# Attention with a parallel SwiGLU gate on one core: pacing the FFN groups, filling TensorE lulls with zero-weight matmuls, and splitting the first statistics

## The chip, the core and the metric

The kernel runs on one core of a Trainium2 chip. The metric is the device time of one execution in microseconds, as the median of several runs. The engines are named as in the profile: PE (TensorE matmul), PEld (weight load), DVE (VectorE), ACT (ScalarE), POOL (GpSimd), SP (SyncE, which issues most DMAs).

## The reference

The input `x` has 2048 tokens of width 512, in bf16. It is layer-normalised once; the result feeds an attention block with 32 query heads of width 16 that share one key and one value head, and a SwiGLU FFN with hidden width 1792. The attention's output is gated with the silu of the FFN's output and added to `x`.

```python
xn = layernorm(x)
q = (xn @ wq) as 32 heads of 16;  k = xn @ wk;  v = xn @ wv
s = (softmax(q k^T / 4) v, heads joined) @ wo
f = (silu(xn @ w_gate) * (xn @ w_up)) @ w_down
out = x + s * silu(f)
```

## The kernel before

The queries are cut into 4 chunks of 512 tokens, the heads into 4 groups of 8. A pair (chunk, head group) has two halves, and a half of a pair is a *block*: 32 blocks in all. A block handles 4 heads against 16 key tiles of 128 keys. For each key tile and each two heads there is one *tile* of scores, 128 keys by 1024 (two heads of 512 queries), so there are 1024 tiles.

Scores are made by PE with 32-row matmuls, two for a tile (`sc_emit`, L814), into one of three 1024-wide PSUM rings. Rings 0 and 1 go to ACT, which turns a tile into probabilities with one exponential (L865). Ring 2 goes to DVE, which makes an approximate exponential in four instructions for two tiles (L892 per tile, then L905, L908, L910 per pair of tiles). 778 tiles go to ACT and 246 to DVE. The product with the values (PV, `pv_emit`, L697) is a *column group*: four 32-column matmuls, one for each head, accumulated in the bank `o_ps` over a block. At the end of a block DVE copies the bank to SBUF (`oev`, L710). The matmul that comes last in the emission carries the stop flag, and the copy waits for all of the block's PV groups.

Between these, PE works off column groups of another kind (`grp_pe`, `cmm`, L466): the gate and up projections (`g_ffn`), the down projection (`g_down`), the q projections of later pairs (`g_q`) and the output projections of finished chunks (`g_out`). All of them use the one bank `m_ps`, whose next user waits for `m_rel`. A gate column block has a tanh on ACT (L608, L625 for the down projection), and multiplications on DVE.

The order on every engine is made in advance, by a planner that runs when the kernel is built. It keeps a clock for each engine with assumed durations (an exponential 0.904 us, a column group 0.215 us), picks the next operation, and at the end emits all operations in the order of their planned starts, chained on each engine. On the chip each engine follows that order; only semaphores decide when. `pump` decides when a job (an FFN column block, a q projection, an output projection) becomes available; `pe_pick` decides what PE does next: a score tile for ACT (`ts`), another ready operation (`tm`, chosen by `rank`), or a score tile for DVE (`td`). Before the DVE share begins, gaps of PE are filled with junk matmuls into an unused bank (L1102). `F0` and `F1` are the tile numbers between which the FFN jobs are spread.

At the start, `pro_x` handles a chunk of 512 tokens: DVE takes the mean and variance of four 128-token tiles (L415, L416), POOL the power -1/2 (L422), DVE normalises (L425), PE transposes (L430), and the result is copied to `xnT` (L436). Chunk 0 goes in two steps of two tiles, with the copies on ACT, followed by the k and q projections of 256 tokens each (L439). All of `x` is loaded by SP's queue, the k, q and v weights by ACT's.

At the end, chunk 3 has no time to go through the usual output path. `g_part` queues the output projection of its four token tiles over the first three head groups, 12 column groups into four banks, once all 1024 tiles are issued. `g_h0` normalises the first half of the last pair by transposes on PE (L940) and three DVE instructions (L948 to L950). The same is done for the second half after the last block's copy; then come two more transposes with a copy on ACT (L1179, L1181), the last quarter of the projection, and the gating and addition (L641, L646). A range check of the denominators and of `v` (`g_checks`, L970 to L974) leads to a flag that would start an exact second path at the end; with this data it does not run.

Of the kernel before, what the change touches and what calls it, by code (L numbers as in the profile page):

```python
# [8 lines left out]
FP32 = mybir.dt.float32  # L9
BF16 = mybir.dt.bfloat16  # L10
# [4 lines left out]
ALU = mybir.AluOpType  # L15
# [17 lines left out]
F_ON, F_OFF = 26, 60  # L33
PB_URG, R_FILL = 6, 0.8
TOL, MERGE = 0.12, 0.1
# [233 lines left out]
def kernel(  # L269
# [64 lines left out]
    def sb(shape, dtype, name):  # L334
        return wp.tile(shape, dtype, name=name)
# [33 lines left out]
    dn = sb([P, NPAIR, GRP], FP32, "dn")  # L369
    rc = sb([P, NPAIR, GRP], FP32, "rc")  # L370
    dscr = [dpool.tile([8, 512], FP32, name=f"dscr{i}") for i in range(2)]
    o_tok = sb([P, 4, P], BF16, "o_tok")
    dl = sb([P, 2, 4, 4, 1], FP32, "dl")
    rd = sb([P, 2, 4, 4, 1], FP32, "rd")
    dlc = sb([P, 32], FP32, "dlc")
    fmin = sb([P, 4], FP32, "fmin")
    fm2 = sb([P, 2], FP32, "fm2")

# [8 lines left out]

    for n in range(0, 4, 2):
        nc.sync.dma_start(out=x_sb[:, n:n + 2, :], in_=x_v[:, n:n + 2, :])
    with nc.allow_non_contiguous_dma(reason="tiny k/v weight loads (32B rows)"):  # L390
# [3 lines left out]
    for c in range(1, NSC):  # L394
# [6 lines left out]
    COEF = (CE, CW)  # L401
    nc.vector.memset(QB[1][:], 0.0)
    chain("POOL", nc.gpsimd.tensor_copy(out=wk_rep[:].rearrange("p k (r d) -> p k r d", d=DH),
                                        in_=wk_sb[:].rearrange("p k (o d) -> p k o d", o=1).to_broadcast(
# [93 lines left out]
    def pro_x(c, pr, banks, ev_eng):  # L498
        arrive = ext(XARR[min(c, 7)])
        step, pk = (2, 1) if c == 0 else (4, 2)  # L500
        evs, grp = [], []
        for n0 in range(4 * c, 4 * c + 4, step):
            st = None
            for n in range(n0, n0 + step):
                st = OP("DVE", 0.77, [arrive, st], lambda n=n: e_stats(n), (pr, n, 0), name="stat")
            v = OP("DVE", 0.08, [st], lambda a=n0, b=n0 + step: e_veps(a, b), (pr - 0.07, n0, 1), name="veps")
            r = OP("POOL", 0.7 + 0.08 * (step - 2), [v], lambda a=n0, b=n0 + step: e_rstd(a, b), (0,), name="rstd")
            for n in range(n0, n0 + step):
                xo = OP("DVE", 0.33, [r, xr_rel[n % 4]], lambda n=n: e_xn(n), (pr - 0.15 if c == 0 else pr - 0.05, n),
                        name="xn")  # L510
                bk = banks[n % 4 // pk]
                h = n % pk
                t_ = OP("PE", 0.26, [xo, brel[bk]] + grp, lambda n=n, bk=bk, h=h: e_tr(n, bank[bk], h), (pr, n), "f",
                        "tr")
                xr_rel[n % 4] = t_
                grp = grp + [t_]
                if len(grp) == pk:
                    ev = OP(ev_eng, 0.5 if ev_eng == "ACT" else 0.34 if pk == 1 else 0.6, grp,
                            lambda n=n, bk=bk: e_txe(n + 1 - pk, pk, bank[bk], ev_eng), (pr - 0.1, n), name="txe")
                    if c:  # L520
                        held.append((grp[0], ev, bk))
                    grp = []
                    brel[bk] = ev
                    evs.append(ev)
        return evs
# [137 lines left out]
    def norm_pair(pair, d0, d1, ev1):  # L663
# [3 lines left out]
        def pack():  # L667
            return [nc.sync.dma_start(out=o0[GRP * g + DH:GRP * g + GRP, :], in_=o1[GRP * g + DH:GRP * g + GRP, :])
                    for g in range(4)]
        pk = OP("DMA", 2.4, [d0, ev1], pack, (0,))  # L670
        r = OP("DVE", 0.26, [d0, d1], lambda: nc.vector.reciprocal(out=rc[:, pair, :], in_=dn[:, pair, :]), (2.2,),
               name="recip")
        sc_ = dscr[pair % 2]
        w = OP("DMA", 2.2, [r], lambda: nc.sync.dma_start(out=sc_[:].rearrange("h (c q) -> (h c) q", q=GRP),
                                                          in_=rc[:, pair, :]), (0,))
        rbt = rb[pair % 2]
# [64 lines left out]

    pair_blk = []

# [189 lines left out]
    F0, F1 = min(F_ON, NTILE), max(NTILE - F_OFF, min(F_ON, NTILE) + 1)  # L933
    job = {"f": 0, "acc": 0.0, "q": 1, "o": 0, "chk": False, "h0": False, "part": False}
    LB = NBLK - 1
# [40 lines left out]

    def g_part():
        order = sorted((0, 1), key=lambda i: slot[i].seq)
        st["late"], st["last"] = order
        bks = ["2a", "2b", "m", f"{order[0]}a"]  # L980
        st["obank"] = bks
        for n, bk in enumerate(bks):
            rel = slot[2] if bk[0] == "2" else (m_rel[0] if bk == "m" else slot[order[0]])
            for jj in range(NQ - 1):
                OP("PE", MMF, [rel, o_ready3()], lambda n=n, bk=bk, jj=jj: e_out_mm(LN + n, bank[bk][:, :D], [jj]),
                   (3,), "c", "part")

    def o_ready3():
        return kb_ready.get(("mul", NPAIR - 2))

    def pump(now):
# [7 lines left out]
        if job["f"] == len(ffn_list) and not job["h0"] and planned([oev.get(LB - 1)]):  # L999
            job["h0"] = True  # L1000
            g_h0()
            return
        if job["h0"] and not job["part"] and p == NTILE and cur["pair"] is None:
            job["part"] = True
            g_part()
            return
# [6 lines left out]
        if n < 4 * (NSC - 1) and n // 4 in o_ready and planned([o_ready[n // 4], g_ready.get(n)]) \  # L1013
# [3 lines left out]
            return  # L1017
        if job["f"] < len(ffn_list) and job["acc"] / tot * (F1 - F0) + F0 <= p:
            w, fn = ffn_list[job["f"]]
            job["f"] += 1  # L1020
            job["acc"] += w
            fn()

    def pe_pick():
# [20 lines left out]
        if ready:  # L1045
# [6 lines left out]
            def rank(o):  # L1052
# [7 lines left out]
                if o.name == "part":  # L1060
                    return (4, o.prio)
                return (R_FILL, (o.seq,))
            co = min(now, key=lambda o: (rank(o), o.seq))
# [20 lines left out]
        if junk and T - F > 0.3:  # L1084
            return F, ("junk", None)
        if ts is not None and ts <= T + 1e-9:
            return ts, ("act", i)
# [7 lines left out]
    def pe_do(start, what):  # L1095
        kind, arg = what
        if kind == "op":
            sd.run(start, arg)
            return
        if kind == "junk":  # L1100
# [65 lines left out]
    def tadd(eng, ins):  # L1166
        chain(eng, ins)

    la, lb = st["late"], st["last"]
    tq01, tq23 = ring[lb][:, 0:512], ring[lb][:, 512:1024]  # L1170
    tp = [ring[la][:, 512:1024], o_ps[:]]
    tadd("PE", tq_emit(1, [0, 1], tq01))
    tadd("PE", tq_emit(1, [2, 3], tq23))
    oTl = oT[(NSC - 1) % 2]
    for h, src in ((0, tq01), (1, tq23)):
# [13 lines left out]
    for k in range(2):  # L1189
        tadd("PE", e_out_mm(LN + k, obk[k], [NQ - 1]))  # L1190
    tadd("PE", nc.tensor.transpose(out=tq01[0:1, 0:P], in_=fmin[:, 3:4], identity=ident_f[:]))
    for k in range(2, 4):
# [9 lines left out]
    tadd("DVE", e_out_mul(LN + 1, obk[1], dsts[1]))  # L1202
    tadd("DVE", nc.vector.tensor_reduce(out=fm2[0:1, 0:1], in_=tq01[0:1, 0:P], axis=AX.X, op=ALU.min))
    tadd("DVE", e_out_mul(LN + 2, obk[2], dsts[2]))
    fin_add(2, nc.gpsimd, "POOL")
    tadd("DVE", nc.vector.tensor_single_scalar(out=fm2[0:1, 1:2], in_=fm2[0:1, 0:1], scalar=0.5, op=ALU.is_lt))
    fin_add(1, nc.vector, "DVE")
    tadd("DVE", nc.vector.tensor_copy(out=flag_i[:], in_=fm2[0:1, 1:2]))
    tadd("DVE", e_out_mul(LN + 3, obk[3], dsts[3]))
# [38 lines left out]
```

## Time and profile before

| | before |
|---|---|
| median of 8 runs | 793.44 us (791.13 to 795.14) |
| profiled execution: time | 796.25 us |
| profiled execution: span, first to last instruction | 794.5 us |
| mean granted TensorE clock | 0.977 |
| busy: PE / DVE / ACT / POOL | 723.9 / 740.8 / 757.5 / 51.3 us |
| ACT exponentials (L865) | 778, 737.1 us |
| scores on PE (L814) | 2048 matmuls, 319.1 us |
| PV groups on PE (L697) | 1556 + 492 + 492 matmuls |

A row of the costliest groups gives line, engine, operation, tiles and shapes, then the count, the busy time, the mean of one, and the idle time of the engine ahead of it with what ended it. Successive ACT instructions overlap in their records, so the mean of one is longer than the distance between two; the distance is taken from their starts. The ends of matmuls are modelled. In a view by windows each engine has its busy time in the window and the number of its instructions; the granted clock is a share of full speed.

### The profile page before, as it was taken

The numbers are of one execution on the slowest core, as the hardware profiler recorded it, in microseconds if no ns is written. First come the engines' busy times: TensorE is split into PE (matmuls) and PEld (weight loads), VectorE is DVE, ScalarE is ACT, GpSimd is POOL, SyncE is SP. The second block draws the span as 40 slices with busy tenths as digits, with TensorE's granted clock in tenths as the row PEclk, the third lists the DMA queues.
The fourth block names the chain that finished last, engine by engine and source line by source line (L and its number), as shares of the span: only waits on it lengthen the run. The fifth ranks groups of instructions, "written<-read, shape, count | busy, mean of one in ns | idle before, by whom it ended". The sixth has DMA issues, their size and how long they took to land.

```text
span 794.5 us, 19255 instructions
## 1 busy us (share of the span) xinstructions
PE 723.9 (91%) x7968; PEld 217.0 (27%) x7968; DVE 740.8 (93%) x925; ACT 757.5 (95%) x860; POOL 51.3 (6%) x59
## 2 busy tenths in 40 slices
PE   8988899999899899998999899999999989999984
PEld 3322222222222222222222222222222222222221
DVE  7789999999999999999999989999999999999983
ACT  5899999999999999999999989999999999999991
POOL 3200000000012000000003000000001100000001
PEclk9899999999999999999999989999999999999996
DMA  9300000000010000000000000000001000000001
GB/s 331 109 2 7 17 2 23 1 10 15 2 30 22 22 2 8 17 1 23 3 22 22 16 14 2 23 2 8 17 2 29 21 23 2 9 16 1 23 1 31
DMA packets 19463, 18.49 MB, mean 23 GB/s; under 512 B 8552, under 2 KB 15464, under 8 KB 19368
## 3 DMA queue, kind: packets, MB, share of 16 engines
q1 hardware_dynamic: 17496, 16.37, 6.8%
q8 instruction: 64, 1.05, 0.6%
q10 hardware_dynamic: 1872, 0.82, 0.4%
q14 instruction: 31, 0.25, 0.1%
HBM read 12.62 MB, written 2.34 MB: 19 GB/s over the span
## 4 chain that ended last, share of the span: by engine, by line
PE 36%; ACT 29%; DVE 22%; issue 8%; DMA 1%; SPq 1%; POOL 0%; DVEq 0%; ACTq 0%
ACT Pb L865 24%; PE ring L814 15%; PE m_ps L466 13%; DVE Ub L892 8%; PE o_ps L697 7%; DVE Wb L910 4%; ACT th L608 4%; DVE Wb L905 3%; DVE Eb L908 2%; ACT th L625 1%; SPq L724 1%; DMA dn<-oa 1%; DVE stats L415 1%; DVE ab L610 1%; DVE ab L641 1%
## 5 line engine op out<-in xcount | busy, mean ns | idle before, releaser
L865 ACT ACTIVATE Pb<-ring 128x1024 bf16<-128x1024 f32 x778 | 737.1, 1171 | 12.1 <-PE ring L814 11.5
L814 PE MATMUL ring<-QB,KT 32*128 32x512 bf16 x2048 | 319.1, 384 | 46.3 <-ACT Pb L865 40.6
L892 DVE TENSOR_SCALAR Ub<-ring 128x1024 uint16<-128x1024 f32 x246 | 299.5, 1218 | 15.6 <-PE ring L814 10.9
L814 PEld LDWEIGHTS <-KT 32*128 32x128 bf16 x2048 | 104.6, 91 | 356.9 <-issue 352.8
L910 DVE TENSOR_TENSOR Wb<-Wb,Ub 128x2048 f16<-128x2048 f16 x123 | 151.2, 1230 | 0.0
L697 PE MATMUL o_ps<-Pb,VA 128*32 128x512 bf16 x1556 | 150.3, 391 | 0.2 <-DVE oa L710 0.2
L905 DVE TENSOR_SCALAR Wb<-Ub 128x2048 uint16<-128x2048 uint16 x123 | 87.5, 712 | 0.3
L908 DVE TENSOR_SCALAR Eb<-Ub 128x2048 uint16<-128x2048 uint16 x123 | 86.9, 709 | 0.0
L466 PE MATMUL m_ps<-xnT,wg_sb 128*32 128x512 bf16 x896 | 74.7, 391 | 0.6 <-DVE QB L593 0.5
L466 PE MATMUL m_ps<-wd_sb,hT 128*32 128x512 bf16 x896 | 72.9, 383 | 0.5 <-DVE g_sb L627 0.5
L466 PE MATMUL m_ps<-xnT,wu_sb 128*32 128x512 bf16 x896 | 71.4, 392 | 0.7 <-DVE ab L610 0.6
L682 POOL TENSOR_TENSOR oT<-oa,rb 128x512 bf16<-128x512 f32 x15 | 21.2, 1410 | 622.4 <-DMA rb<-dscr 387.7
L697 PE MATMUL o_ps<-Eb,VD 128*32 128x512 f16 x492 | 48.9, 387 | 5.4 <-DVE Eb L908 4.3
L697 PEld LDWEIGHTS <-VA 128*32 128x32 bf16 x1556 | 37.9, 94 | 53.8 <-issue 53.4
L697 PE MATMUL o_ps<-Wb,VD 128*32 128x512 f16 x492 | 49.0, 388 | 2.2 <-DVE Wb L910 1.7
L697 PEld LDWEIGHTS <-VD 128*32 128x32 f16 x984 | 29.2, 94 | 48.2 <-issue 47.1
L608 ACT ACTIVATE th<-m_ps 128x512 f32<-128x512 f32 x56 | 41.6, 743 | 0.0
L614 DVE TENSOR_TENSOR hT<-ab,m_ps 128x512 bf16<-128x512 f32 x56 | 38.1, 681 | 2.3 <-PE m_ps L466 2.2
L610 DVE SCALAR_TENSOR_TENSOR ab<-th,m_ps 128x512 f32<-128x512 f32 x56 | 38.1, 680 | 1.3 <-ACT th L608 1.0
L710 DVE COPY oa<-o_ps 128x512 f32<-128x512 f32 (+1 forms) x33 | 22.0, 670 | 9.3 <-PE o_ps L697 9.0
L466 PEld LDWEIGHTS <-wg_sb 128*32 128x32 bf16 x896 | 17.1, 95 | 26.3 <-issue 25.3
L466 PEld LDWEIGHTS <-wu_sb 128*32 128x32 bf16 x896 | 16.1, 95 | 26.3 <-issue 24.3
(94 smaller groups left out, 235.4 us busy)
## 6 DMA issues: line engine op xcount, KB each, us to landing
rb<-dscr SPq DMA_DIRECT2D x15, 256.0 KB
dn<-oa SPq DMA_DIRECT2D x120, 2.0 KB, 1.7
oa<-oa SPq DMA_DIRECT2D x60, 32.0 KB, 2.0
wg_sb<-in_B_w_gate_dram SPq DMA_DIRECT2D x1, 1792.0 KB, 11.4
wu_sb<-in_B_w_up_dram SPq DMA_DIRECT2D x1, 1792.0 KB
wd_sb<-in_B_w_down_dram SPq DMA_DIRECT2D x1, 1792.0 KB, 20.3
out_dram<-xn SPq DMA_DIRECT2D x14, 128.0 KB, 1.7
x_sb<-in_A_x_dram SPq DMA_DIRECT2D x3, 512.0 KB
```

The costliest lines, as they stand in the source:

```text
L466: return [nc.tensor.matmul(out=dst[GRP * j:GRP * j + GRP, :], lhsT=w[:, GRP * j:GRP * j + GRP], rhs=rhs, start=start, stop=stop, tile_posi ...
L608: t_ = OP("ACT", 0.477, [a], lambda: nc.scalar.activation(out=th[i][:], in_=m_ps[:], func=ACT.Tanh, scale=0.5), (0,), name="tanh")
L610: s_ = OP("DVE", 0.6, [t_, ab_rel[i]], lambda: nc.vector.scalar_tensor_tensor(out=ab[i][:], in0=th[i][:], scalar=1.0, in1=m_ps[:], op0=ALU ...
L614: h = OP("DVE", 0.6, [b], lambda: nc.vector.tensor_tensor(out=hT[:, f, :], in0=ab[i][:], in1=m_ps[:], op=ALU.mult), (1,), name="hmul")
L697: r.append(nc.tensor.matmul(out=o_ps[GRP * g:GRP * g + GRP, :], lhsT=lhs, rhs=rhs, start=(n == 0), stop=(n == pv_total[(b, g)] - 1), tile_ ...
L710: oev[b] = sd.new(_Op("DVE", 0.6, [], lambda: [nc.vector.tensor_copy(out=oat[:, a:z], in_=o_ps[:, a:z]) for a, z in cuts], (0.2,), name="o ...
L814: return lambda: [nc.tensor.matmul(out=ring[sl][:, u * 512:(u + 1) * 512], lhsT=KT[half][GRP * g:GRP * g + GRP, t * P:(t + 1) * P], rhs=QB ...
L865: lambda: nc.scalar.activation(out=Pb[pi][:], in_=ring[i][:], func=ACT.Exp, scale=escale, bias=ebias),
L892: lambda: nc.vector.tensor_scalar(out=Ub[ui][:, x * 1024:(x + 1) * 1024], in0=ring[2][:], scalar1=ubias, scalar2=UINF, op0=ALU.add, op1=AL ...
L905: o1 = OP("DVE", 0.6, [pa, pa0, w_rel[u - NE] if u >= NE else None], lambda: nc.vector.tensor_scalar(out=Wb[ei][:], in0=Ub[ui][:], scalar1 ...
L908: o2 = OP("DVE", 0.6, [pa, pa0, e_rel[u - NE] if u >= NE else None], lambda: nc.vector.tensor_scalar(out=Eb[ei][:], in0=Ub[ui][:], scalar1 ...
L910: o3 = OP("DVE", 1.135, [o1, o2], lambda: nc.vector.tensor_tensor(out=Wb[ei][:].bitcast(FP16), in0=Wb[ei][:].bitcast(FP16), in1=Ub[ui][:]. ...
```

## The change

- **Start.** The second half of chunk 0 of `x` is loaded by ACT's queue, ahead of the weights, instead of SP's. Its statistics are made by ACT: two copies that accumulate the sum, the mean, two squares of `x - mean` that accumulate the variance, with `hT` as a scratch output. DVE then makes `veps` from the sums. The first half stays on DVE.
- **Pacing.** `ahead()` is the number of FFN column groups queued beyond the even spread. An FFN job becomes available as soon as this is 16 or less (`AHEAD`), where before it had to be zero or less. While it is 8 or more (`LAZY`), the rank of such groups goes from 0.8 to 3.5, behind PV.
- **Zero groups.** In `pe_pick`, if the next planned start is at least one column group away and fewer than seven (`ZN`) column groups started in the last 3.4 us of planned time, a column group with weights `zw` (all zero) and the first 512 tokens of `xnT` is put into the PV bank of the open block, provided that the block has begun and has PV groups still to come.
- **Tail.** The partial projection goes into four separate pieces: token tiles 0 and 1 (bank of ring 2) are made available when the last DVE tile is issued, tile 2 (`m_ps`) after the half-0 normalisation is queued, tile 3 after the last transposes.
- **Flag.** The minimum over the partitions is replaced by a matmul with a column of ones, and the flag is one comparison instead of three DVE instructions.
- **Reciprocals.** `rc` keeps two slots instead of one for each pair.

```diff
-PB_URG, R_FILL = 6, 0.8
+PB_URG, AHEAD, LAZY, ZN = 6, 16, 8, 7
...
-    for n in range(0, 4, 2):
-        nc.sync.dma_start(out=x_sb[:, n:n + 2, :], in_=x_v[:, n:n + 2, :])
+    nc.sync.dma_start(out=x_sb[:, 0:2, :], in_=x_v[:, 0:2, :])
+    nc.scalar.dma_start(out=x_sb[:, 2:4, :], in_=x_v[:, 2:4, :])
...
+            if c == 0 and n0 == 2:
+                a = None
+                for n in (2, 3):
+                    a = OP("ACT", 0.55, [arrive, a], lambda n=n: nc.scalar.activation(
+                        out=hT[:, n, :], in_=x_sb[:, n, :], func=ACT.Copy, accum_out=ssum[:, n - 2:n - 1]), (-1,),
+                        name="asum")
+                a = OP("ACT", 0.2, [a], lambda: nc.scalar.activation(
+                    out=mv[:, 2:4, 0], in_=ssum[:, 0:2], func=ACT.Copy, scale=1.0 / D), (-1,), name="amean")
+                for n in (2, 3):
+                    a = OP("ACT", 0.55, [a], lambda n=n: nc.scalar.activation(
+                        out=hT[:, n, :], in_=x_sb[:, n, :], func=ACT.Square, scale=-1.0, bias=mv[:, n, 0:1],
+                        accum_out=ssum[:, n:n + 1]), (-1,), name="asq")
+                v = OP("DVE", 0.08, [a], lambda: nc.vector.tensor_scalar(
+                    out=veps[:, 2:4], in0=ssum[:, 2:4], scalar1=1.0 / D, scalar2=EPS, op0=ALU.mult, op1=ALU.add),
+                    (pr - 0.07, n0, 1), name="veps")
...
-    def g_part():
...
+    def g_part(n):
+        bk = st["obank"][n]
+        rel = slot[2] if bk[0] == "2" else m_rel[0]
+        for jj in range(NQ - 1):
+            OP("PE", MMF, [rel, o_ready3()], lambda jj=jj: e_out_mm(LN + n, bank[bk][:, :D], [jj]), (3,), "c", "part")
...
+    def ahead():
+        return job["acc"] - (cur["issued"] - F0) * tot / (F1 - F0)
...
-        if job["h0"] and not job["part"] and p == NTILE and cur["pair"] is None:
+        if not job["part"] and act_block() in (LB, None) and cur["pair"] is None and dve_tile(0) is None \
+                and planned([o_ready3()]):
             job["part"] = True
-            g_part()
+            g_part(0)
+            g_part(1)
+        if job["h0"] and not job["partm"] and planned([o_ready3()]):
+            job["partm"] = True
+            g_part(2)
...
-        if job["f"] < len(ffn_list) and job["acc"] / tot * (F1 - F0) + F0 <= p:
+        if job["f"] < len(ffn_list) and ahead() <= AHEAD:
...
-                return (R_FILL, (o.seq,))
+                return (0.8 if ahead() < LAZY else 3.5, (o.seq,))
...
+        zb = act_block()
+        zb = NBLK - 1 if zb is None else zb
+        if not junk and cur["issued"] >= D_START and T - F >= MMF + sd.switch("c") \
+                and sum(1 for q in c_log[-ZN:] if q > F - 3.4) < ZN:
+            for bb in (zb - 1, zb):
+                if bb >= 0 and oev[bb].start is None and oev[bb - 1].start is not None \
+                        and sd.avail(oev[bb - 1], "PE") <= F and blk_pv[bb] and blk_pv[bb][0].start is not None \
+                        and oev[bb].left > 0 and any(o.start is None for o in blk_pv[bb]):
+                    return F, ("zero", bb)
...
+        if kind == "zero":
+            o = _Op("PE", MMF, [oev[arg - 1]], pv_emit(arg, [(zw[:], xnT[:, 0, 0:512], g) for g in range(4)]), (0,), "c",
+                    "zero")
...
     tadd("PE", tq_emit(1, [2, 3], tq23))
+    tadd("PE", e_out_mm(LN + 3, bank[st["obank"][3]][:, :D], range(NQ - 1)))
...
-    tadd("PE", nc.tensor.transpose(out=tq01[0:1, 0:P], in_=fmin[:, 3:4], identity=ident_f[:]))
+    tadd("PE", nc.tensor.matmul(out=tq01[0:1, 0:1], lhsT=fmin[:, 3:4], rhs=ones_f[:], start=True, stop=True))
...
-    tadd("DVE", nc.vector.tensor_reduce(out=fm2[0:1, 0:1], in_=tq01[0:1, 0:P], axis=AX.X, op=ALU.min))
...
-    tadd("DVE", nc.vector.tensor_single_scalar(out=fm2[0:1, 1:2], in_=fm2[0:1, 0:1], scalar=0.5, op=ALU.is_lt))
+    tadd("DVE", nc.vector.tensor_single_scalar(out=flag_i[:], in_=tq01[0:1, 0:1], scalar=P - 0.5, op=ALU.is_lt))
...
-    tadd("DVE", nc.vector.tensor_copy(out=flag_i[:], in_=fm2[0:1, 1:2]))
```

## The prediction

> **What bounds the kernel now.** I read the page first, for the engines' shares and the clock row. ACT is busy 95% of the span, DVE 93%, PE 91%. The clock row is 9 almost everywhere and dips at both ends.
>
> ```profile
> PE 723.9 (91%) x7968; PEld 217.0 (27%) x7968; DVE 740.8 (93%) x925; ACT 757.5 (95%) x860; POOL 51.3 (6%) x59
> PEclk9899999999999999999999989999999999999996
> ```
>
> ACT sets the pace. In the undisturbed stretches its 1024-wide exponentials start 0.915 us apart without a gap, and 778 of them at 0.915 us with 72 tanh steps at 0.49 us come to 747 us. From the first exponential (13.23) to the end of the last (777.23) it is 764.0 us, so about 15 us are lost on ACT in between. Next I cut windows, because the clock row is too coarse. Columns: length, busy time of PE, PEld, DVE, ACT, POOL, granted clock, DMA.
>
> ```profile
> 6.41:9.82 3.41, 2.96 (x22) 1.60 (x21) 3.25 (x13) 1.07 (x2) 1.11 (x3) 1.00 1.15 328
> 306.79:310.20 3.41, 2.41 (x28) 0.74 (x24) 3.41 (x4) 3.41 (x6) 0.00 (x0) 1.00 0.02 5
> 310.20:313.61 3.41, 3.41 (x32) 0.49 (x24) 2.64 (x4) 2.54 (x4) 0.00 (x0) 0.50 0.02 2
> 402.36:405.77 3.41, 3.41 (x30) 0.66 (x26) 1.84 (x4) 2.91 (x5) 0.00 (x0) 0.50 0.01 1
> 463.80:467.21 3.41, 2.52 (x28) 0.78 (x20) 3.41 (x5) 3.41 (x5) 0.47 (x1) 1.00 0.00 0
> 467.21:474.04 6.83, 6.83 (x52) 1.11 (x50) 6.21 (x7) 4.64 (x5) 0.00 (x0) 0.50 0.01 2
> 774.41:781.24 6.83, 6.40 (x56) 2.22 (x59) 0.76 (x2) 2.82 (x4) 0.00 (x0) 0.50 0.01 2
> ```
>
> Three times in mid-kernel the granted clock falls to 0.50 for one or two windows of 3.41 us; each time the window before held few column groups (sets of four 32-column matmuls). It falls again at the very end. In the half-clock windows PE is full and ACT has holes: the bound moves from ACT to PE. ACT's timeline there, with the idle time before each row:
>
> ```profile
> 467.43 1.02 ACT L865 ACTIVATE Pb<-ring 128x1024 bf16<-128x1024 f32 x1 [0.22 <-PE ring L814]
> 468.94 1.02 ACT L865 ACTIVATE Pb<-ring 128x1024 bf16<-128x1024 f32 x1 [0.49 <-PE ring L814]
> 470.46 1.02 ACT L865 ACTIVATE Pb<-ring 128x1024 bf16<-128x1024 f32 x1 [0.49 <-PE ring L814]
> ```
>
> The exponentials come 1.51 us apart instead of 0.915, so each loses 0.6. Summing what exceeds 0.915 (0.49 after a tanh) from the starts gives 1.3 us around 310, 0.9 around 402 and 2.9 around 467: 5.1 us for the three drops. The rest of the 15 us is 5.6 before 45 us, where the clock is 0.50 from 16.65 to 26.89, and 4.5 in scattered stalls.
>
> **Start: half the statistics of chunk 0 to ACT.** The chain of the second half of chunk 0:
>
> ```profile
> 7.39 0.69 DVE L415 BATCH_NORM_STATS2 stats<-x_sb 128x6 f32<-128x512 bf16 x1
> 8.59 0.71 POOL L422 TENSOR_TENSOR rstd<-veps,neg_half 128x2 f32<-128x2 f32 x1 [1.77 <-DVE veps L419]
> 9.33 0.74 DVE L425 TENSOR_SCALAR xn<-x_sb,mv,rstd 128x512 bf16<-128x512 bf16 x2
> 13.23 1.02 ACT L865 ACTIVATE Pb<-ring 128x1024 bf16<-128x1024 f32 x1 [0.48 <-PE ring L814]
> ```
>
> DVE loses two stats (0.69) and two aggregates (0.18). ACT, idle here until 7.97, gets four 512-wide passes and a tiny one. Accumulating activations are not in the trace; the nearest row is ACT's 512-wide copy (two in 1.07 us). Data by 4.2 (issued at 0.72, 3.5 us to landing), four passes at 0.54, 0.2 for the mean and about 0.2 for handovers end at 6.8. Then veps 0.2, POOL 0.71 behind its other power and the k-weight copy. That copy starts about 0.5 later, since the k-weight load now stands behind the x load on ACT's queue; its memsets (1.1 together) push the first power from 5.82 to about 6.2, which is covered because the second ends last. xn of the second half starts near 8.3 instead of 9.33: 1.0 us gained. Twice the copy's time per pass would put ACT at 9.0 and lose 1.2; in DVE's order xn of tiles 0 and 1 now stands behind the veps that waits for ACT, so nothing would cover that.
>
> Against it stands the clock. In the window 6.41 to 9.82 the old program had five full-width junk matmuls beside eight transposes. The new PE order has one junk matmul ahead of the first scores where the old one had nine, and sixteen transposes in a row. If the clock halves there, the sixteen 256-column q and k matmuls (0.107 each by the pitch of the old rows) double, 1.7 us, nearly all of it on this path. Ends +1.0 and -0.7; I take a gain of 0.4, a little above the middle, because the row with the nearest load stayed at 1.00.
>
> The Trainium skill ("TensorE: Matmul & The Clock Gate", Part 4: PE-mode transpose) says that transposes don't count as PE-busy for the clock. No row here has transposes alone. By that rule the start would be the -0.7 and the sum below 1.1 us higher.
>
> **Middle: pacing and zero groups.** A column group may now be queued up to 16 ahead and steps back behind everything when 8 ahead, so the same 1296 groups of the FFN and projections are spread. Where PE still has a lull with fewer than seven groups in 3.4 us, a zero-weight group is put into the open PV bank: 148 matmuls, 37 groups. Exponentials (778), DVE tiles (246) and all evacuations keep their counts. I counted, in both program orders, the places after the first tiles where four ACT tiles in a row have five column groups or fewer: ten before (and the tail), six after. The drops of the trace fell at exponentials 298, 392 and 459; the first two are such places. At two hits in ten places, six places give 1.2 drops where the trace had three; at 1.7 us each 2.0 us stay of 5.1. Gain 3.1; ends 0 and 5.1.
>
> The zero groups cost PE time: consecutive groups stand 0.22 us apart, so 8.1 us in all. PE is recorded busy 671.92 of 725 us between 45 and 770, and the groups go only where the planner sees a hole; the planner counts 0.904 per exponential where the chip takes 0.915, so holes are longer than planned. Bounds 0 and 8.1; I take 0.3, near the hiding end. The last PV evacuation of a block now waits for its zero groups too, but these precede the block's last PV in PE's order.
>
> The skill speaks against this part: the same page ("HAM oscillation — how this bites in real kernels") states as its rule that no PE-idle gap should exceed about 3.4 us. No such gap exists here: PE was busy 2.41 and 2.52 us of the windows ahead of two drops, and the clock fell. The measurement decides: a sparse window is enough. By the rule alone the zero groups would buy nothing and the 3.1 would fall away.
>
> **Tail: the partial out-projection.** The old tail:
>
> ```profile
> 768.59 8.64 ACT L865 ACTIVATE Pb<-ring 128x1024 bf16<-128x1024 f32 x9
> 776.38 2.78 PE L466 MATMUL ring<-wo_sb,oT 128*32 128x512 bf16 x24
> 778.94 0.64 PE L697 MATMUL o_ps<-Pb,VA 128*32 128x512 bf16 x4
> 779.64 0.76 DVE L710 COPY oa<-o_ps 128x256 f32<-128x256 f32 x2 [6.42 <-PE o_ps L697]
> 781.69 0.66 PE L940 MATMUL ring<-ident_f,oa 128*128 128x128 f32 x4
> 782.45 0.17 DVE L948 COPY dl<-ring 128x8 f32<-128x8 f32 x1 [2.06 <-PE ring L940]
> ```
>
> ACT ends at E = 777.23. The last PV stands behind six half-clock out-projection groups, the transposes behind six more, and DVE reads them at E+5.22. In the new order the last PV stands first, then nine groups, then the transposes; the last three groups come after these, where PE waited 0.89 us for o_tok anyway. But the half-0 normalisation (0.17, 0.25, 0.42) now follows the last PV evacuation on DVE, and the m_ps groups wait for it. With a full clock: PV at E+0.2, evacuation E+0.9 to E+1.7, normalisation to E+2.6, three groups (0.65), transposes and handover (0.76): DVE reads at E+4.1. That is 1.1 gained. With a half clock nine groups at 0.43 put it at E+5.3: nothing. The final-flag steps lose two small DVE operations (0.2 and 0.06 on the serial chain). Since the last FFN tanh now stands four ACT steps from the end instead of ten, the last windows are dense and I take the full clock: 1.4 with the flag; ends -0.1 and 1.9.
>
> **Sum.** The profiled execution took 796.25 us, span 794.5 and 1.75 around it. 796.25 - 0.4 - 3.1 + 0.3 - 1.4 = 791.65. It stands 2.8 above the median of 793.44. I read that as drops: the fastest run, 791.13, is the profiled one less the 5.1. So a median run holds about 2.3 us of drops (an estimate), of which the same six tenths, 1.4, go; with the other three terms (-1.5) that is 790.5 us.
>
> **Rivals.** First, the sparse windows only move: six places remain, and the start goes cold. Then the drops stay, the start gives -0.7, the tail 1.4: 793.44 + 0.7 + 0.3 - 1.4 = 793.0. For it: ten such places gave only two hits, so places and drops are loosely tied; against it: four-tile stretches with six groups or fewer fall from 91 to 34. Second, slower: PE is in order, and each zero group or pushed-back FFN group that the chip reaches late stands ahead of the next score pair, which ACT awaits. All 37 late cost 8.1 us: 793.44 - 2.9 + 7.8 = 798.3. It decides from about 21 late groups on (4.5 us: the 2.9 gained and the 1.6 that can be told). For it: PE already makes ACT wait at 15 exponentials after 45 us; against it: those waits sum to 6.3 us and most lie in the drops. Third, better: no drop at all and the full 1.0 at the start, 793.44 - 2.3 - 1.0 + 0.3 - 1.4 = 789.0, or less if spreading also removes some of the 4.5 of scattered stalls.
>
> **Chances.** Forecast 0.52, better 0.14, moved windows 0.22, slower 0.12. About 0.2% (1.6 us) is what a measurement of this kernel can tell from no change. So faster 0.66, same 0.22, slower 0.12. The range runs from 787.3, some of the scattered stalls gone, to 794.8, where the slower case has barely begun.
>
> **What would show it.** Right: no 0.50 windows, or one, between 45 and 770; ACT busy in nearly every window; the first exponential at 12.2 to 13.0; DVE's first read of the last transposes about 4.1 us after ACT's end at clock 1.00. Wrong: half-clock windows near exponentials 82, 108, 131, 322, 472 or 662; ACT waiting for scores right behind zero groups; an ACT statistics chain ending past 8 us; a half clock between 9 and 13 us.

## The result, and the profile after

The change made the kernel slower: 799.07 us median of 21 runs (790.37 to 805.53) against 792.70 of 58 runs of the kernel before on the same chips; ratio 1.0056, 95% interval [1.0036, 1.0076]. The ratios here and below leave out runs that are over 1.5% slower than the fastest of their kernel (6 of 23 of the changed kernel), while medians keep them. The forecast was 790.5. The profiled execution of the changed kernel is one of its fastest, 791.36 us with a span of 789.6, so its trace shows where things stand and not how much a usual run loses; for the sizes the runs are used.

The page, first the shares and then the clock row:

```profile
PE 730.0 (92%) x8110; PEld 222.0 (28%) x8110; DVE 738.0 (93%) x921; ACT 758.9 (96%) x869; POOL 49.0 (6%) x59
PEclk9999999899999999999999999999999999999998
```

PE is busy 6.1 us longer, the zero groups among it. Windows of the changed kernel around half clock (length, busy PE, PEld, DVE, ACT, POOL, granted clock, DMA):

```profile
5.28:8.69 3.41, 1.22 (x6) 0.37 (x4) 1.32 (x8) 2.10 (x7) 2.41 (x7) 1.00 1.05 346
8.69:12.10 3.41, 2.80 (x21) 2.35 (x22) 2.85 (x8) 2.04 (x4) 0.73 (x2) 0.50 1.11 362
121.34:124.75 3.41, 2.15 (x24) 0.71 (x20) 3.15 (x5) 3.41 (x5) 0.00 (x0) 1.00 0.04 7
124.75:128.16 3.41, 3.41 (x28) 0.64 (x26) 2.00 (x4) 2.65 (x3) 0.00 (x0) 0.50 0.19 39
145.23:148.64 3.41, 2.34 (x24) 0.91 (x21) 3.41 (x5) 3.41 (x6) 0.00 (x0) 1.00 0.01 1
148.64:155.47 6.83, 6.82 (x50) 1.21 (x53) 5.33 (x7) 4.91 (x6) 0.00 (x0) 0.50 0.02 3
660.64:664.05 3.41, 2.47 (x24) 0.71 (x25) 3.26 (x5) 3.41 (x5) 0.00 (x0) 1.00 0.03 4
664.05:667.46 3.41, 3.41 (x30) 0.63 (x22) 1.81 (x4) 2.36 (x4) 0.00 (x0) 0.50 0.03 5
```

The drops in mid-kernel are not gone. They stand at exponentials 108, 131 (half clock from 148.64 to 155.47) and 662: three of the six sparse places that the prediction named. In each of the three sparse windows DVE copies the PV bank at a block's end (at 121.47, 145.73 and 660.76). The start goes cold from 8.69 to 12.10, where the old program had full clock. The start in the timeline (start, length, idle time before the row in brackets):

```profile
4.32 0.63 ACT L510 ACTIVATE hT<-x_sb 128x512 bf16<-128x512 bf16 x1 [1.58 <-DMA x_sb<-in_A_x_dram]
4.86 0.19 ACT L510 ACTIVATION_READ_ACCUMULATOR hT<-x_sb 128x1 f32 x1
...
6.28 0.61 POOL L407 COPY wk_rep<-wk_sb 128x512 bf16<-128x512 bf16 x1 [4.93 <-DMA wk_sb<-in_A_wk_dram]
...
7.47 0.34 DVE L519 TENSOR_SCALAR veps<-ssum 128x2 f32<-128x2 f32 x1 [1.28 <-ACT hT L516]
...
8.52 1.54 DVE L429 TENSOR_SCALAR xn<-x_sb,mv,rstd 128x512 bf16<-128x512 bf16 x4 [0.71 <-POOL rstd L426]
...
14.08 2.90 ACT L887 ACTIVATE Pb<-ring 128x1024 bf16<-128x1024 f32 x3 [0.57 <-PE ring L836]
```

All four normalisations now wait to 8.52; the old program had the first two at 6.75. The first exponential comes at 14.08, not 13.23. The tail, in the same view:

```profile
771.55 3.14 ACT L887 ACTIVATE Pb<-ring 128x1024 bf16<-128x1024 f32 x3
...
774.74 0.39 PE L719 MATMUL o_ps<-Pb,VA 128*32 128x512 bf16 x2 [0.20 <-ACT Pb L887]
775.17 0.76 DVE L732 COPY oa<-o_ps 128x256 f32<-128x256 f32 x2 [0.38 <-PE o_ps L719]
...
778.34 0.17 DVE L970 COPY dl<-ring 128x8 f32<-128x8 f32 x1 [1.02 <-PE ring L962]
```

ACT ends at E = 774.69, and DVE reads the last transposes at E+3.65, where the old program did so at E+5.22. The clock is full in this stretch. The tail works.

### The profile page after: what moved, and what is told of

It reads as the page before. It is cut to its first block, busy times and chain, and to the rows that moved or that the text cites. A ratio compares the mean times of both kernels' runs of the same rounds, so it can differ in the third digit from the quotient of the medians.

```text
span 789.6 us, 19554 instructions
## 1 busy us (share of the span) xinstructions
PE 730.0 (92%) x8110; PEld 222.0 (28%) x8110; DVE 738.0 (93%) x921; ACT 758.9 (96%) x869; POOL 49.0 (6%) x59
## 4 chain that ended last, share of the span: by engine, by line
PE 48%; ACT 29%; DVE 12%; issue 7%; DMA 2%; SPq 1%; ACTq 0%; DVEq 0%
ACT Pb L887 23%; PE ring L836 20%; PE m_ps L470 18%; PE o_ps L719 9%; ACT th L630 5%; DVE Ub L914 4%; DVE Wb L932 2%; DMA wv_sb<-in_A_wv_dram 2%; ACT th L647 1%; DVE Wb L927 1%; DVE Eb L930 1%; SPq L746 1%; DVE oa L732 1%; DMA dn<-oa 0%; DMA oa<-oa 0%
## 5 line engine op out<-in xcount | busy, mean ns | idle before, releaser
L836 PEld LDWEIGHTS <-KT 32*128 32x128 bf16 x2048 | 110.2, 91 | 348.9 <-issue 345.1
L930 DVE TENSOR_SCALAR Eb<-Ub 128x2048 uint16<-128x2048 uint16 x123 | 84.3, 688 | 0.0
L470 PE MATMUL m_ps<-xnT,wu_sb 128*32 128x512 bf16 x896 | 73.3, 396 | 0.8 <-DVE ab L632 0.8
L630 ACT ACTIVATE th<-m_ps 128x512 f32<-128x512 f32 x56 | 43.4, 775 | 0.0
## 6 DMA issues: line engine op xcount, KB each, us to landing
wg_sb<-in_B_w_gate_dram SPq DMA_DIRECT2D x1, 1792.0 KB, 11.2
wd_sb<-in_B_w_down_dram SPq DMA_DIRECT2D x1, 1792.0 KB, 20.5
```

Source lines behind the costliest of these rows:

```text
L470: return [nc.tensor.matmul(out=dst[GRP * j:GRP * j + GRP, :], lhsT=w[:, GRP * j:GRP * j + GRP], rhs=rhs, start=start, stop=stop, tile_posi ...
L630: t_ = OP("ACT", 0.477, [a], lambda: nc.scalar.activation(out=th[i][:], in_=m_ps[:], func=ACT.Tanh, scale=0.5), (0,), name="tanh")
L836: return lambda: [nc.tensor.matmul(out=ring[sl][:, u * 512:(u + 1) * 512], lhsT=KT[half][GRP * g:GRP * g + GRP, t * P:(t + 1) * P], rhs=QB ...
L930: o2 = OP("DVE", 0.6, [pa, pa0, e_rel[u - NE] if u >= NE else None], lambda: nc.vector.tensor_scalar(out=Eb[ei][:], in0=Ub[ui][:], scalar1 ...
```

## The experiments

**How the runs are read.** Each run lists its mean granted clock, and with it its half-clock time: (1 - clock) / 0.5 x time. Within a version a run's time follows it closely: over 273 runs of all versions, each taken from its version's mean, 0.32 us are lost for each us of half clock (correlation 0.95). So a version has two parts: its half-clock time, the mean over all its runs, and a *rest*, its mean time less 0.32 of that. *Wait* is the idle time of DVE ahead of the reciprocals in the one profiled execution, which the second group of experiments is about. A ratio compares with runs of the kernel before on the same chip; the row of the kernel before holds its runs in all of these jobs.

| version | median us (runs) | ratio to before, 95% | half clock us | rest us | wait us |
|---|---|---|---|---|---|
| before | 793.40 (98, all jobs) | | 35.2 | 782.5 | 4.3 |
| after | 799.07 (21) | 1.0056 [1.0036, 1.0076] | 42.7 | 785.2 | 5.8 |
| no_zero | 802.48 (6) | 1.0103 [1.0067, 1.0140] | 60.6 | 784.5 | 3.8 |
| zero_only | 796.59 (12) | 1.0035 [1.0007, 1.0063] | 34.3 | 786.3 | 11.2 |
| start_only | 797.82 (12) | 1.0055 [1.0026, 1.0085] | 48.3 | 783.0 | 3.6 |
| tail_only | 791.58 (12) | 0.9959 [0.9937, 0.9982] | 31.0 | 780.6 | 4.5 |
| pace_only | 791.41 (12) | 0.9967 [0.9937, 0.9997] | 24.7 | 783.4 | 4.7 |
| tiny_w | 796.64 (12) | 1.0035 [1.0003, 1.0068] | 33.1 | 785.8 | 8.4 |
| start_q | 796.58 (12) | 1.0047 [1.0016, 1.0078] | 44.5 | 782.5 | 3.4 |
| start_book | 793.45 (12) | 1.0000 [0.9975, 1.0025] | 31.9 | 783.2 | 3.9 |
| before_late | 784.54 (6) | 0.9894 [0.9858, 0.9930] | 18.3 | 778.7 | 0 |
| zero_late | 784.50 (7) | 0.9879 [0.9843, 0.9915] | 18.4 | 778.9 | 0 |
| tail_late | 783.45 (7) | 0.9867 [0.9826, 0.9908] | 26.0 | 778.4 | 0 |
| tz_late | 783.69 (6) | 0.9875 [0.9840, 0.9910] | 16.7 | 778.3 | 0 |
| after_late | 791.56 (12) | 0.9965 [0.9940, 0.9990] | 31.4 | 781.1 | 0 |
| after_late_book | 783.08 (6) | 0.9878 [0.9832, 0.9923] | 16.5 | 778.2 | 0 |
| book_6p5 | 794.74 (12) | 1.0021 [0.9995, 1.0047] | 42.7 | 780.6 | 0 |
| book_1p2 | 810.99 (6) | 1.0207 [1.0152, 1.0263] | 65.2 | 789.7 | 17.0 |

**The parts one by one.** Four kernels: the change without its zero groups, and the kernel before with one part alone (the zero groups; the start; the tail with the flag). zero_only and tail_only also have the two slots of `rc`; and without zero groups the pacing acts in no_zero, so that its plan differs from the changed kernel's by more than the groups.

```diff
 no_zero (from after)
-PB_URG, AHEAD, LAZY, ZN = 6, 16, 8, 7
+PB_URG, AHEAD, LAZY, ZN = 6, 16, 8, 0
 zero_only, start_only, tail_only (from before)
+ the hunks of that part alone
```

> The changed kernel without its 37 zero groups (the limit ZN is 0); start split, tail and flag stay. The theory 'zero groups cost' (they push real column groups apart or don't keep the clock up): the loss goes, 791 to 793 us, mean granted clock up from about 0.972 to 0.98 or more. The theory 'the start costs' (the statistics on ACT come late and begin the first windows at half clock): nothing gets better, 798 to 800 us, clock near 0.97. The theory of the prediction (zero groups mend sparse windows): worse than the changed kernel, over 800 us.

> The kernel before with the zero groups alone (36 groups; the old start, tail and pacing; two reciprocal slots). 'Zero groups cost': about 799 to 801 us at a clock near 0.97, as the changed kernel without its tail gain of 1.6. 'The start costs': 791 to 793 us at 0.98 or more. The prediction's theory: 789 to 791 us.

> The kernel before with the split of the first statistics alone (ACT for tiles 2 and 3, x loaded by two queues). 'Zero groups cost': first exponential 0.9 us later than before as in the trace of the changed kernel, so 793 to 795 us. 'The start costs': 799 to 801 us at a clock near 0.97.

> The kernel before with the new tail and flag alone (the pieces of the partial projection after the last PV, a ones matmul for the flag, two reciprocal slots; no zero groups, old start, old pacing). Both theories: 1.0 to 1.9 us faster than before, about 791 us, clock unchanged. If it is slower, the tail is a third cause.

By the ratios, against a kernel of 793 us: tail -3.3 us, zero groups +2.8, start +4.4; together +3.9 where the whole change has +4.4. The tail gains, as was forecast, and more. The start loses through the clock: its rest is near that of before (783.0 against 782.5), its half-clock time 13.1 us longer. In its trace the half clock comes twice, from 8.42 to 15.25 and from 18.66 to 25.49, and then holds from 39.14 to 59.62. Here are its first exponential in the timeline, and the last of these stretches by windows, first in start_only, then in the kernel before:

```profile
15.47 1.02 ACT L884 ACTIVATE Pb<-ring 128x1024 bf16<-128x1024 f32 x1 [0.96 <-PE ring L833]
```

```profile
39.14:59.62 20.48, 20.00 (x142) 4.85 (x138) 10.72 (x14) 13.99 (x16) 0.81 (x3) 0.50 0.00 1
39.14:59.62 20.48, 18.17 (x206) 5.76 (x205) 17.08 (x22) 20.48 (x24) 0.81 (x3) 1.00 0.01 2
```

ACT gets 16 instructions into this stretch where it had 24. The zero groups alone leave the half-clock time as it was (34.3) and lose 3.8 us in the rest. Without them the whole change holds half clock for 60.6 us and is no faster (802.48, six runs); whether the groups save drops there or another plan makes them, no_zero doesn't tell.

**Pacing.** Planned with the old pacing, the changed kernel has the same order of instructions on every engine: with the zero groups in PE's time the planner's queue of FFN groups runs behind the even spread, so the new thresholds don't act. One run had the pacing alone.

> The kernel before with the new pacing of the FFN groups (up to 16 ahead, step back behind everything at 8 ahead) and nothing else of the change. In the whole change the order of instructions is the same with the old pacing; alone it draws another plan, with six places that have five column groups or fewer in four exponentials where the kernel before has eleven. Theory A (the places matter little beside the waits): 791.5 to 794.5, no difference. Rival B (spreading the groups saves the drops of the clock): 789 to 791.

791.41, at the edge between the two theories: rest 0.9 us above before, 10.5 us less half clock. By itself the pacing is worth about 0.3%; in this change it does nothing.

**What the zero groups cost.** At the end of a block, once DVE has copied the PV bank (`oa<-o_ps`), SP issues four 2 KB DMAs that collect the denominators in `dn`, and for each pair DVE takes their reciprocal (`rc<-dn`). The planner books 2.4 us for these DMAs. Here is a block end of zero_only in the timeline, and two windows of the same place:

```profile
171.37 2.40 SPq L726 DMA_DIRECT2D dn<-oa  x4
...
176.97 0.35 DVE L673 RECIPROCAL rc<-dn 128x32 f32<-128x32 f32 x1 [2.56 <-DMA dn<-oa]
177.24 0.63 DVE L911 TENSOR_SCALAR Eb<-Ub 128x2048 uint16<-128x2048 uint16 x1
...
177.92 0.62 PE L699 MATMUL o_ps<-Eb,VD 128*32 128x512 f16 x4 [2.15 <-DVE Eb L911]
...
179.60 1.02 ACT L868 ACTIVATE Pb<-ring 128x1024 bf16<-128x1024 f32 x1 [2.44 <-PE ring L817]
```

```profile
174.30:177.72 3.42, 1.47 (x18) 0.50 (x15) 0.86 (x3) 2.86 (x4) 0.00 (x0) 1.00 0.16 34
177.72:181.13 3.41, 3.21 (x26) 0.63 (x29) 2.43 (x4) 1.03 (x2) 0.00 (x0) 0.50 0.18 43
```

The chain reads downwards. The reciprocal stands at the head of DVE's queue and DVE idles 2.56 us; `Eb` behind it is late; PE, in order, idles 2.15 for `Eb` with score pairs behind it; ACT idles 2.44; PE was busy only 1.47 us of the window, and the clock halves. What stood ahead of the scores was a PV group that waited for DVE, not a zero group. The same comes again at the drop at 648.76, so two of the three drops of this trace between 45 and 768 us follow such a wait:

```profile
647.85 0.35 DVE L673 RECIPROCAL rc<-dn 128x32 f32<-128x32 f32 x1 [2.43 <-DMA dn<-oa]
```

```profile
645.35:648.76 3.41, 1.36 (x18) 0.50 (x15) 0.98 (x3) 2.91 (x4) 0.00 (x0) 1.00 0.14 30
648.76:655.59 6.83, 6.26 (x44) 1.15 (x47) 5.72 (x7) 3.22 (x4) 1.27 (x1) 0.50 0.16 46
```

In the order of instructions the reciprocals moved closer behind the copies: summed over the pairs, they stand 101 DVE instructions behind them, where the old order has 122.

Three versions then book 4.2 us for the four DMAs: the zero groups alone, the new tail alone, and the two together. The edit is one number:

```diff
-        dens_op[b] = OP("DMA", 2.4, [ev], dens, (0,))
+        dens_op[b] = OP("DMA", 4.2, [ev], dens, (0,))
```

> The kernel before with the 36 zero-weight groups alone, and one number of the planner raised: it now books 4.2 us, not 2.4, for the four small DMAs that carry a block's denominators, and so places the reciprocal that waits for them later in VectorE's order. With zero groups alone VectorE stood 11.1 us at these reciprocals (4.3 before) and the time was 796.6 us against 793.1. Theory A (the 3.5 us are VectorE standing at the head of its queue for a transfer that the plan thought shorter): the reciprocal waits fall under 3 us and the time to 792.0 to 793.5. Rival B (the zero groups cost their own PE time in front of score pairs): waits may fall, but the time stays at 796 to 797.

> The kernel before with the new tail alone (791.6 us) and the same raised booking of 4.2 us for the denominators' DMAs. Without zero groups VectorE stood only 4.5 us at the reciprocals, 5 times. Theory A: these few waits go, of which ScalarE had felt at most 1 to 2 us, so 790.0 to 791.5 us, unless the newly drawn plan has more sparse windows (11 places with five column groups or fewer in four exponentials against 11). Rival B (the booking has nothing to do with the time): 791.6, within 1 us.

> New tail, 36 zero groups and the booking of 4.2 us, with the start and the pacing as in the kernel before: the version that the parts point to. In its order of instructions three places, not six as with the booking of 2.4 us, have five column groups or fewer within four exponentials. Theory A: tail 791.6, zero groups at no cost once the waits at the reciprocals are gone, and half-clock time of 25 to 31 us as against 31.0: 789.5 to 791.0 us. Rival B (zero groups cost their own 3.5 us whatever the booking): 794.5 to 795.5.

All waits are gone, and all three fall to 783.5 to 784.5, lower than either theory had it. With the right booking the zero groups cost nothing that these runs can tell (784.50 against 784.54 without, before_late below; 783.69 against 783.45 with the new tail), and they gain nothing either: half clock 18.4 against 18.3. The next runs put the one number into the kernel before and into the whole change.

> The kernel before, with nothing changed but the planner's booking of the four denominator DMAs, 4.2 us for 2.4. With the new tail this one number took 791.6 us to 783.5, with zero groups 796.6 to 784.5. Theory A (the reciprocal at the head of VectorE's queue, and the planned times that run ahead of the chip behind it, are a cost of the kernel before itself): 783.5 plus the 1.8 of the old tail, 784 to 787. Rival B (the gain needs the new tail or the zero groups): 791 to 793.5.

> The whole change, with the booking of 4.2 us for the denominators. Theory A (what the change lost beyond its start was the wait at the reciprocals): with the tail 1.8 faster, zero groups at no cost, and the start's 4 to 5 us still in it, 786 to 790 against 799.1 for the change as it is. Rival B (the change's loss lies elsewhere): 795 or more.

Theory A holds for before_late. after_late is 1.6 us above its range. The last run below, with the start's queue and bookings repaired, has 783.08; so the start held 8.5 us there, with the plan that it draws.

How much of this is the wait, and how much the plan drawn anew? With 4.2 us the planner also gave DVE two tiles more (776 exponentials on ACT, 248 tiles on DVE). Two other bookings leave 778:

> The kernel before, the booking of the denominator DMAs at 6.5 us. The order of instructions is another than with 4.2, and ScalarE keeps 778 exponentials where 4.2 left it 776 (two more tiles went to VectorE: 1.8 us of ScalarE). Theory A (the gain of 8 to 9 us was the wait at the reciprocal with what follows from it, and at most 1.8 of it the two exponentials): no wait, 784.5 to 788. Rival B (a lucky plan): 790 to 794.

> The kernel before, the booking at 1.2 us: in VectorE's order 71 instructions stand between the evacuations of the blocks and their reciprocals, 122 with 2.4, 101 in the version with zero groups. Theory A: VectorE waits longer than the 11 us of the version with zero groups, and the time is 796 to 800. Rival B: 791 to 794.

The rows of the waits, in us, times and the longest, for zero_only and book_1p2:

```profile
DVE rc L673 <- DMA dn<-oa: 8.1, 5, 2.6
```

```profile
DVE rc L671 <- DMA dn<-oa: 15.9, 11, 2.2
```

book_1p2 came out far slower, beyond even theory A's range. book_6p5 speaks for B, and the table shows why both are half right. Its rest, 780.6, is 1.9 us below before, as for a kernel without waits; but its plan holds half clock for 42.7 us, and that takes 2.4 back. Over the nine versions with the old tail and 778 exponentials the rest is 780.8 us plus 0.53 us for each us of wait (correlation 0.99). So the wait is priced: 4.3 us of it cost the kernel before about 2.2, and 11.2 cost zero_only 5.9, 3.7 more, which covers the 3.8 that it lost in the rest. The two with 776 exponentials, before_late and zero_late, lie about 2 us below this line, the size of two exponentials. So of the 9.2 us by which before_late's mean is lower, about 2 are the wait, about 2 the two exponentials that DVE took over, and 5.4 are half-clock time of the plan. Every plan with 776 exponentials and without the change's own start has 26 us of that or less, every plan with 778 but pacing alone has 31 or more. What in the plan does that was not settled.

**Does a multiplication by zero count for the clock?** The same plan as zero_only with weights that are not zero:

```diff
-    nc.vector.memset(zw[:], 0.0)
+    nc.vector.memset(zw[:], 1e-20)
```

> The kernel before with the 36 added groups alone, their weights 1e-20 instead of 0 (the sums don't change); same order of instructions as with zero weights. Theory A (the added groups stand in windows that were dense anyway): half clock for 30 to 39 us as with zeros (34.3) and 795 to 798.5. Rival B (a multiplication by zero doesn't count for the clock): fewer drops, half clock 20 to 27 us, 791 to 794.

Half clock 33.1 us against 34.3, time 796.64 against 796.59: theory A's numbers. This alone doesn't show that a zero counts, since most groups stand where no drop threatened: of the 36 zero groups of zero_only's trace, 26 stand in windows that have five or more other groups. The windows of all the traces do show it (3.41 us, full clock, between 45 and 768 us). After windows with three or four column groups and no added one the clock fell in 42 of 148 cases; after those with three or four and one to three zero-weight groups beside them it fell in none of 51. So a zero-weight group counts, but it can't go where it is needed. It needs an open PV bank, and of the seven windows with four groups or fewer that are left in zero_only's trace, six lie within 4 us of the copy at a block's end.

**The start.** Two steps: x back on SP's queue, so that the k weights come first again; then also the passes of ACT booked at their measured length.

```diff
 start_q (from start_only)
-    nc.sync.dma_start(out=x_sb[:, 0:2, :], in_=x_v[:, 0:2, :])
-    nc.scalar.dma_start(out=x_sb[:, 2:4, :], in_=x_v[:, 2:4, :])
+    for n in range(0, 4, 2):
+        nc.sync.dma_start(out=x_sb[:, n:n + 2, :], in_=x_v[:, n:n + 2, :])
 start_book (from start_q)
-                    a = OP("ACT", 0.55, [arrive, a], lambda n=n: nc.scalar.activation(
+                    a = OP("ACT", 0.82, [arrive, a], lambda n=n: nc.scalar.activation(
...
-                    a = OP("ACT", 0.55, [a], lambda n=n: nc.scalar.activation(
+                    a = OP("ACT", 0.91, [a], lambda n=n: nc.scalar.activation(
```

> The kernel before with the split of chunk 0's statistics over ScalarE and VectorE, but all of x on SyncE's queue as before, so that the k weights are again first on ScalarE's queue. Its order of instructions on each engine is that of the split alone (797.8 us, half clock for 48 us in the mean of its runs, first exponential at 15.47 us). Theory A (the k weights behind x delay the powers and with them the whole start): the spread of k weights on GpSimd begins near 4.1 us, not 6.3, the first exponential near 13.5 to 14.3, half clock falls to 34 to 40 us and the time to 793 to 795. Rival B (the sums on ScalarE and the order that the plan drew around them are the cause, not the queue): 797 to 798.5.

> The kernel before with the split of chunk 0's statistics, x on SyncE's queue as before, and ScalarE's passes booked at what they took in the trace (0.82 and 0.91 us with the read of the accumulator, for 0.55). In VectorE's order the normalisation of tokens 0 and 1 then stands ahead of the veps that waits for ScalarE; with 0.55 it stands behind it, and VectorE idled 2.25 us there. Theory A (the start lost by this order): the first normalisation starts near 6.8 us, not 8.5, the first exponential at 12.8 to 13.5, not 14.4, and the time goes from 796.6 to 791.5 to 793.5. Rival B (the plan drawn anew, or the sums on ScalarE themselves, cost the 4 us): 795 to 798.

The timeline of start_q with the k-weight copy, two rows of DVE and the first exponential; then DVE's rows and the first exponential of start_book:

```profile
4.18 0.61 POOL L404 COPY wk_rep<-wk_sb 128x512 bf16<-128x512 bf16 x1 [2.83 <-DMA wk_sb<-in_A_wk_dram]
...
8.12 0.17 DVE L516 TENSOR_SCALAR veps<-ssum 128x2 f32<-128x2 f32 x1 [2.25 <-ACT hT L513]
...
8.51 1.37 DVE L426 TENSOR_SCALAR xn<-x_sb,mv,rstd 128x512 bf16<-128x512 bf16 x4
...
14.41 1.94 ACT L884 ACTIVATE Pb<-ring 128x1024 bf16<-128x1024 f32 x2 [0.48 <-PE ring L833]
```

```profile
6.64 0.73 DVE L426 TENSOR_SCALAR xn<-x_sb,mv,rstd 128x512 bf16<-128x512 bf16 x2 [0.55 <-POOL rstd L423]
...
8.13 0.17 DVE L516 TENSOR_SCALAR veps<-ssum 128x2 f32<-128x2 f32 x1 [0.76 <-ACT hT L513]
...
13.40 2.86 ACT L884 ACTIVATE Pb<-ring 128x1024 bf16<-128x1024 f32 x3 [0.48 <-PE ring L833]
```

The queue is the smaller part: the k-weight copy starts at 4.18, not 6.46, the first exponential comes at 14.41, not 15.47, but the time falls by 1.2 us only (0.6 by the ratios, inside the noise) and stays above theory A's 793 to 795. The bookings are the rest, 3.7 us by the ratios, as theory A had it. With 0.55 booked, `veps<-ssum` stands ahead of the normalisation of token tiles 0 and 1, and DVE idles 2.25 us with work behind it; with the true lengths it stands behind, the first exponential comes at 13.40, half clock falls from 44.5 to 31.9 us, and the time is that of the kernel before. Where these 12.6 us of half clock went the traces don't show: both have 20.5 us of it before 60 us, and the rest of the plan is drawn anew too. The split then costs nothing and brings nothing: ACT's chain ends at 8.1, so the second pair of token tiles is normalised at 9.13, where the old program had 9.33.

Last, the whole change with both bookings and the queue repaired:

> The whole change with both bookings repaired (denominators 4.2 us, ScalarE's passes 0.82 and 0.91) and x on SyncE's queue. Theory A: the start's loss gone as well, so as fast as the version without the start change (783.7) or up to 1 us faster: 781.5 to 784.5. Rival B (the start costs whatever is booked): 787 to 789.

It is the fastest median of all, 783.08, within the intervals of tail_late and tz_late. Its page:

```profile
PE 729.9 (93%) x8115; PEld 223.2 (29%) x8115; DVE 743.2 (95%) x926; ACT 757.0 (97%) x867; POOL 49.8 (6%) x59
```

## Why the prediction was wrong

- **Start (forecast -0.4, ends +1.0 and -0.7 of gain).** The step that failed most. The order was seen ("xn of tiles 0 and 1 now stands behind the veps that waits for ACT"), and set aside because ACT's chain was sized at 0.54 us a pass. A pass took 0.61 to 0.72 with a second instruction of 0.19 behind it, and the chain ended at 7.45 for a forecast of 6.8. The Trainium skill ("VectorE: DVE Perf Modes", Two Vector instructions with no wait between them) says for VectorE that an operation with an accumulator output is two instructions; the ACT rows above show the same there. The k-weight copy was put 0.5 us later and came 2.2 later (6.28 against 4.06). The larger miss is that the working ended at the first exponential. start_only is 2.2 us late there (15.47 against 13.23) and loses 4.4 us in all: its half-clock time is 13.1 us longer, 4.2 us at 0.32, in its trace up to 60 us into the kernel, which no term held. The sixteen transposes were not what chilled the start: they come after 8.69, and the window ahead of the half clock held 1.22 us of PE work, since PE waited for the late `xn`.
- **Middle, the drops (-3.1).** Failed: half clock 34.3 us with zero groups alone, and on average no less in the whole change than before. Counting places was a fair guide to where the clock falls, three of six hit, but not to how often: in six traces (before, after and the first four experiments) it fell after 3 of 3 full-clock windows with two column groups, 11 of 16 with three, 5 of 38 with four, 1 of 158 with five and none of over 1000 with more. The groups went to other windows: in the changed kernel's trace all three drops stand at block ends, where no group can go. In zero_only two of three followed a wait of DVE, which a count in the order of instructions can't show. As to the skill's rule ("TensorE: Matmul & The Clock Gate", HAM oscillation), no gap of 3.4 us stands ahead of these drops either: 2.15 and 2.47 us busy were sparse enough.
- **Zero groups' cost (+0.3, bounds 0 and 8.1).** The measured +2.8 (rest +3.8) lies inside the bounds, but by another way than PE's own time: the plan that they draw puts the reciprocals too early. The slower rival had groups in front of score pairs; that was not it, and that its 798.3 lies near the measured 799.07 is luck.
- **Tail and flag (-1.4).** Right, by its own steps: DVE reads at E+3.65 for a forecast of E+4.1, and tail_only is 3.3 us faster by the ratio: 1.9 in the rest, just at the far end of the forecast, and the other 1.4 in 4.2 us less half clock, which was not forecast.
- **The marks.** Half clock between 9 and 13 us, drops at the named exponentials and a first exponential past 13.0 said "wrong" as they should; the chain past 8 us did not (it ended at 7.45), so that mark was set too late.
- **Slips in the numbers.** 764.0 less 747 leaves 17 us lost on ACT, not 15. The pitch of the exponentials is 0.904 us at the median of the trace and not 0.915, so the planner's 0.904 was no reason for longer holes. The FFN and the projections have 796 column groups (3184 matmuls), not 1296. None of these decides the outcome.

The first rival, windows that move and a cold start, described the trace best; it gave 793.0 because it priced the cold start by its 0.7 us alone.

## What to carry to other kernels

Where a planner fixes the order ahead of time, a duration booked too short is not a small error: the consumer comes to the head of an in-order queue and everything behind it waits, here through three engines into the clock. So before adding work to fill holes, compare the booked durations with the trace, above all for DMAs and for instructions that the hardware splits; one number, 4.2 for 2.4, moved the same kernel by more than the whole change did. And an edit to such a kernel is priced with the plan that it draws, not by the edited instructions alone: a booking of 6.5 us took the waits away as well, and its plan was no faster than before.

## What the runs showed of the hardware

- The four 2 KB DMAs are issued by SP 0.63 us apart at the median (0.55 at the least), and a reciprocal that waited for them started 3.63 to 5.62 us after the copy had ended (eleven traces).
- Half clock can last though PE is busy: in start_only from 39.14 to 59.62, with PE busy 20.00 of 20.48 us. Where it comes in mid-kernel, exponentials come 1.51 us apart for 0.90, which would lose 0.40 us per us; the runs lose 0.32.
- Column groups with zero weights counted for the granted clock: it fell after none of 51 full-clock windows of 3.41 us that held three or four other groups and at least one of these, and after 42 of 148 without.
